# Normalizing attention in groups of three, and converting early weights inside the attention loop

## The chip, the cores and the metric

The kernel runs on one core of a Trainium2 chip. The metric is the time of one execution on the device, in microseconds. Before the change the median of three runs is 826.88 us (826.86 to 827.37). The core's engines run side by side, each through its own list of instructions in order: TensorE (PE: matmuls; PEld: its weight loads), VectorE (DVE), ScalarE (ACT), GpSimd (POOL) and SyncE (SP), which here only issues DMAs. An instruction that reads what another engine writes waits for a semaphore, and everything behind it on its engine waits too.

## The reference

An attention in which a query sees only the keys of its own bucket, and two layers of gated experts behind it. Inputs of the second part are 64-bit floats.

```python
q_bits = (einsum('bhsd,dk->bhsk', q, proj) > 0)      # 6 bits: the bucket; k_bits likewise
mask = q_bucket[:, :, :, None] == k_bucket[:, :, None, :]
scores = where(mask, scale * q @ k.T, -1e9)          # 2 x 8 heads, 768 x 768, head size 64
attn = exp(scores - max(scores)); attn /= attn.sum(-1) + 1e-09
x = (attn @ v) as 1536 tokens x 512
x = (sigmoid(x @ w_gate) * (x @ w_val)) @ w_out      # inner size 1536
h = x @ w_in; out = (h * cos(h)) @ w_out             # inner size 2048
```

A row of `attn` whose bucket holds no key becomes uniform, 1/768.

## The kernel before

**Attention.** A head has 6 groups of 128 query rows, so there are 96 groups `g`. One pass of the loop at `for g in range(NG + LAG + 2)` is a *step*: it works on several groups at once, each in another stage, and within a step the list `ORDER` (in the first steps `FILL`) gives the order in which the stages issue their instructions. That order is final, since the scheduler is told to keep it. The stages of a group:

- `S`: four matmuls write the scores (`scores`, L399 and L402), two steps ahead of the group's own step, negated, with the mask added as a large number by extra rows of the matmul; `MIN`: their row minimum on VectorE (`rowmax`, L406);
- `COEF` (L411): one VectorE operation turns the minimum into scale and bias of the exponential, (-1, minimum), or (0, 0) for a row without a key; `EXP` (L425): the exponential on ScalarE, with the row sum beside it;
- `GRD` (L432) and `RCP` (L438): the sum plus 1e-9, and its reciprocal, on VectorE; `NRM` (L442): GpSimd multiplies the group's 128 x 768 values by it, in place;
- for three groups together, LAG steps later, in 6 half steps `w` of 128 keys: `Ta`/`Tb` transposes on TensorE (L451, tile `t`), `HIa`/`HIb` the high part on ScalarE (L456, `ph`), `LOa`/`LOb` the low part on VectorE (L461, `pl`), `PVa`/`PVb` the products with the values on TensorE (L471 and L472, tile `o`).

With `LAG = 5` the step of group g holds the products of half steps 2(g-5) and 2(g-5)+1. `FIN` copies a finished product (`e`, L480) and sends halves of it across partitions by DMA (L486 to L489); once a pair of heads is done, GpSimd adds them (`ef`, L494) behind the second DMA, and ScalarE and GpSimd write high and low part to `xy` (L510, L514).

Beside it the heads ahead are prepared by a table of due steps (`LOAD_AT`, `TRANS_AT`, `BITS_AT`, `VALUES_AT`): loads, transposes (L286), high and low part (L301, L302 and L305, tile `x`), bucket bits (L360, L363) and the values' two parts (L267, L270, tile `vs`). `PREP` starts what is due, `LATE` runs its second half in the next step.

**Weights.** A weight tile of 128 x 512 arrives as 64-bit words. `convert` turns it to 32 bits: one ScalarE operation (L151) and three on VectorE (L153, L156, L165). `wsplit` makes a high part on ScalarE (L123) and a low part on VectorE or GpSimd (L124). The first six tiles (`NEARLY`) are loaded from step 86 on; four are converted in steps 97 to 100, where only products are left, the other two at the beginning of the second part.

**Second part.** Products of gate, value and output weights, all on TensorE (L670, L732, L759). The scheduler keeps the order within each part; where the end of the first meets the beginning of the second it may place the second's instructions among the first's.

Of the kernel before, what the change touches and what calls it, by code (L numbers as in the profile page):

```python
# [39 lines left out]
def lsh_attention_glu_moe_cos_moe(  # L40
# [190 lines left out]
    def attention():  # L231
        with ExitStack() as st:
# [172 lines left out]
            def rowmax(g):  # L405
                nc.vector.tensor_reduce(mm[:, g % NM, 1:2], s_t[g], axis=AX.XY, op=ALU.min)  # L406

            def coef(g):
                m = mm[:, g % NM, :]
                cb = tiny.tile([P, 2], F32, tag="cb", name=f"cb{g}")  # L410
                nc.vector.scalar_tensor_tensor(  # L411
                    out=cb,
                    in0=m[:, 1:2].to_broadcast([P, 2]),
                    scalar=CUT,
                    in1=m,
                    op0=ALU.is_lt,
                    op1=ALU.mult,
                )
                cb_t[g] = cb

            def expo(g):
                pt = pp.tile([P, 2, HS], F32, tag="p", name=f"p{g}")
                sm = tiny.tile([P, 1], F32, tag="sm", name=f"sm{g}")
                cb = cb_t.pop(g)
                nc.scalar.activation(  # L425
# [426 lines left out]
```

## Time and profile before

| | us |
|---|---|
| median of three runs | 826.88 |
| profiled execution, its own time | 826.57 |
| its span, first to last instruction | 824.8 |
| TensorE busy | 798.6 (97%) |
| VectorE busy | 609.1 (74%) |
| ScalarE busy | 469.1 (57%) |
| GpSimd busy | 312.3 (38%) |

Shares are means over parts with different limits: VectorE's 74% is 99% in the attention and less behind it. A matmul's end is modelled, so where TensorE is called busy it may still be held up for a moment; the start of a matmul that comes once in every step shows that better. "Idle before" in a row is time in which the engine stood, with what ended it.

### The profile page before, as it was taken

The numbers are of one execution on the slowest core, as the hardware profiler recorded it, in microseconds if no ns is written. First come the engines' busy times: TensorE is split into PE (matmuls) and PEld (weight loads), VectorE is DVE, ScalarE is ACT, GpSimd is POOL, SyncE is SP. The second block draws the span as 40 slices with busy tenths as digits, with TensorE's granted clock in tenths as the row PEclk, the third lists the DMA queues.
The fourth block names the chain that finished last, engine by engine and source line by source line (L and its number), as shares of the span: only waits on it lengthen the run. The fifth ranks groups of instructions, "written<-read, shape, count | busy, mean of one in ns | idle before, by whom it ended". The sixth has DMA issues, their size and how long they took to land.

```text
span 824.8 us, 12075 instructions
## 1 busy us (share of the span) xinstructions
PE 798.6 (97%) x3984; PEld 676.8 (82%) x3984; DVE 609.1 (74%) x1157; ACT 469.1 (57%) x896; POOL 312.3 (38%) x315
## 2 busy tenths in 40 slices
PE   7999999999986999999999999999999999999998
PEld 5899999899974888888888888887888888868886
DVE  7999999999998255555454357787777777787773
ACT  5899989888985233223222244456666666664442
POOL 5678878777743112111211112131222222222221
PEclk9999999999997999999999999999999999999999
DMA  7676667576515132223222103232333232243212
GB/s 178 144 167 151 148 152 180 124 169 166 153 30 183 41 103 77 76 82 98 96 83 77 41 36 103 90 115 76 103 103 92 89 101 83 97 137 119 86 68 102
DMA packets 69070, 89.06 MB, mean 108 GB/s; under 512 B 29520, under 2 KB 52048, under 8 KB 69008
## 3 DMA queue, kind: packets, MB, share of 16 engines
q1 hardware_dynamic: 68208, 88.10, 37.6%
q8 instruction: 31, 0.51, 0.3%
q14 instruction: 31, 0.25, 0.1%
q10 hardware_dynamic: 800, 0.20, 0.1%
HBM read 59.77 MB, written 3.15 MB: 76 GB/s over the span
## 4 chain that ended last, share of the span: by engine, by line
PE 81%; DVE 9%; issue 3%; ACT 3%; DMA 2%; POOL 1%; SPq 0%; DVEq 0%; POOLq 0%; ACTq 0%
PE a L759 15%; PE ph L670 14%; PE pg L670 12%; PE pv L670 12%; PE a L732 12%; PE t L451 5%; PE o L471 2%; PE o L472 2%; PE s L399 2%; PE s L402 2%; DVE pl L461 2%; PE pb L360 1%; DVE cb L411 1%; DMA e<-e 1%; ACT p L425 1%
## 5 line engine op out<-in xcount | busy, mean ns | idle before, releaser
L670 PE MATMUL ph<-xy,ih 128*128 128x512 f32 x384 | 118.3, 389 | 0.0
L123 ACT CAST gh<-g 128x512 fp32r<-128x512 f32 x84 | 52.1, 620 | 113.4 <-PE a L759 44.8
L124 POOL TENSOR_TENSOR zl<-w_z,zh 128x512 fp32r<-128x512 f32 x32 | 41.8, 1307 | 169.5 <-ACT zh L123 169.5
L425 ACT ACTIVATE p<-s,cb 128x768 f32<-128x768 f32 x96 | 96.1, 1001 | 13.1 <-DVE cb L411 6.8
L456 ACT CAST ph<-t 128x384 fp32r<-128x384 f32 x192 | 90.8, 485 | 16.1 <-PE t L451 12.1
L696 DVE TENSOR_TENSOR g<-pv,sg 128x512 f32<-128x512 f32 x36 | 24.8, 690 | 99.3 <-PE pv L670 99.3
L451 PE MATMUL t<-ident,p 128*128 128x128 f32 x576 | 94.7, 273 | 3.3 <-DVE pl L461 3.2
L461 DVE TENSOR_TENSOR pl<-t,ph 128x384 fp32r<-128x384 f32 x192 | 96.4, 540 | 1.8 <-ACT ph L456 0.8
L442 POOL TENSOR_SCALAR p<-p,r 128x768 f32<-128x768 f32 x96 | 87.0, 908 | 26.1 <-DVE r L438 12.8
L406 DVE TENSOR_REDUCE mm<-s 128x1 f32<-128x768 f32 x96 | 90.7, 945 | 0.5 <-PE s L402 0.5
L670 PE MATMUL pg<-xy,gh 128*128 128x512 f32 x288 | 90.6, 396 | 0.0
L670 PE MATMUL pv<-xy,vh 128*128 128x512 f32 x288 | 89.1, 391 | 0.0
L694 ACT ACTIVATE sg<-pg 128x512 f32<-128x512 f32 x36 | 21.3, 592 | 117.8 <-PE pg L670 117.8
L451 PEld LDWEIGHTS t<-ident,p 128*128 128x128 f32 x576 | 73.8, 140 | 13.9 <-DVE pl L461 6.5
L670 PEld LDWEIGHTS ph<-xy,ih 128*128 128x128 f32 x384 | 72.0, 188 | 15.1
L124 DVE TENSOR_TENSOR gl<-g,gh 128x512 fp32r<-128x512 f32 x84 | 59.8, 714 | 32.7 <-ACT gh L123 30.5
L471 PE MATMUL o<-ph,vs 128*128 128x384 f32 x192 | 80.5, 419 | 1.5 <-ACT e L480 1.5
L759 PE MATMUL a<-zh,gh 128*128 128x512 f32 x192 | 75.0, 391 | 1.1 <-ACT gh L123 0.4
L759 PE MATMUL a<-zl,gh 128*128 128x512 f32 x192 | 75.0, 390 | 0.7 <-POOL zl L124 0.7
L759 PE MATMUL a<-zh,gl 128*128 128x512 f32 x192 | 74.8, 390 | 0.0
L670 PE MATMUL ph<-xy,il 128*128 128x512 f32 x192 | 74.7, 389 | 0.0
L472 PE MATMUL o<-pl,vs 128*128 128x384 f32 x192 | 65.8, 343 | 6.8 <-DVE pl L461 6.8
(107 smaller groups left out, 1860.8 us busy)
## 6 DMA issues: line engine op xcount, KB each, us to landing
raw_z<-in_moe_w_out SPq DMA_DIRECT2D x32, 512.0 KB, 3.2
raw_o<-in_moe_w_out SPq DMA_DIRECT2D x24, 512.0 KB, 3.2
q<-x SPq DMA_DIRECT2D x45, 192.0 KB, 3.1
k<-x SPq DMA_DIRECT2D x45, 192.0 KB, 3.4
raw_i<-in_moe_w_in SPq DMA_DIRECT2D x16, 512.0 KB, 3.8
raw_g<-in_moe_w_gate SPq DMA_DIRECT2D x12, 512.0 KB, 3.5
raw_v<-in_moe_w_val SPq DMA_DIRECT2D x12, 512.0 KB, 3.7
nv<-in_v SPq DMA_DIRECT2D x8, 384.0 KB, 3.5
```

Source lines behind the costliest of these rows:

```text
L124: sub.tensor_tensor(out=dst_l, in0=src, in1=dst_h.bitcast(F32), op=ALU.subtract)
L406: nc.vector.tensor_reduce(mm[:, g % NM, 1:2], s_t[g], axis=AX.XY, op=ALU.min)
L425: nc.scalar.activation(pt, s_t.pop(g), AF.Exp, bias=cb[:, 1:2], scale=cb[:, 0:1], accum_out=sm)
L442: nc.gpsimd.tensor_scalar(out=pt, in0=pt, scalar1=r_t.pop(g), scalar2=1.0, op0=ALU.mult, op1=ALU.mult)
L451: nc.tensor.transpose(pt[:, i, :], pv_[:, j * P : (j + 1) * P], ident)
L456: nc.scalar.copy(ph, pt_t[w])
L461: nc.vector.tensor_tensor(out=pl, in0=pt_t.pop(w), in1=ph_t[w].bitcast(F32), op=ALU.subtract)
L471: nc.tensor.matmul(o_t[u], vs[:, j, :], ph_t.pop(w), start=(j == 0), stop=False)
L472: nc.tensor.matmul(o_t[u], vs[:, j, :], pl_t.pop(w), start=False, stop=(j == T - 1))
L670: nc.tensor.matmul(ps, w[:, kt, :], xy[c][:, hl, kt, :], start=(n == 0), stop=(n == 11))
L732: nc.tensor.matmul(acc[c, e], w[:, e, :], m, start=(f == 0 and n == 0), stop=(f == F1 - 1 and n == 2),)
L759: nc.tensor.matmul(acc[c, t], m[:, ts], w, start=(f == 0 and n == 0), stop=(f == F2 - 1 and n == 2),)
```

## The change

The minimum goes straight into the exponential as its bias, with scale -1. The small operations are done for three groups at once, on tiles of 128 x 3, at the beginning of every third step: the sum plus 1e-9 (`r`), a number `d` that is 1/768 for a row without a key and else 0, the reciprocal, and `r` set to 0 where the row has no key. `NRM` then normalizes three groups one after the other, as `p * r + d`. `LAG` is 7, so products come two steps later; values are loaded and split later in the table; tiles `p` have 10 buffers instead of 8. `convert` becomes a generator that stops twice: from step 26 on, every tenth step starts one of the six early weights, and the next two steps do its other two pieces. Loads begin at step 16.

```diff
 ORDER = (
-    "Tb LOa PVb EXP Ta MIN GRD LATE COEF RCP W HIb PVa S NRM FIN HIa PREP PVaF LOb".split()
+    "Tb LOa COEF PVb EXP Ta MIN LATE W HIb PVa S NRM FIN HIa PREP PVaF LOb".split()
 )
...
-LOAD_AT = {"q": -17, "k": -19, "v": -13}
+LOAD_AT = {"q": -17, "k": -19, "v": -6}
...
-VALUES_AT = (-8, -6)
+VALUES_AT = (-3, -1)
...
-    def convert(key):
+    def convert_parts(key):
...
             out=lt, in0=lw, scalar1=29, scalar2=7, op0=ALU.logical_shift_right, op1=ALU.bitwise_and
         )
+        yield
...
             op1=ALU.bitwise_or,
         )
+        yield
...
-            pp = st.enter_context(tc.tile_pool(name="pp", bufs=8))
-            tiny = st.enter_context(tc.tile_pool(name="tiny", bufs=6))
+            pp = st.enter_context(tc.tile_pool(name="pp", bufs=10))
+            tiny = st.enter_context(tc.tile_pool(name="tiny", bufs=3))
...
+            def expo(g):
+                u, i = divmod(g, 3)
+                pt = pp.tile([P, 2, HS], F32, tag="p", name=f"p{g}")
+                nc.scalar.activation(
+                    pt,
+                    s_t.pop(g),
+                    AF.Exp,
+                    bias=mn_t[u][:, i : i + 1],
+                    scale=-1.0,
+                    accum_out=sm_t[u][:, i : i + 1],
+                )
+                p_t[g] = pt
+
+            def coef(u):
...
+                nc.vector.tensor_scalar(out=r, in0=sm, scalar1=1e-9, scalar2=None, op0=ALU.add)
+                nc.vector.tensor_scalar(
+                    out=d,
+                    in0=mn,
+                    scalar1=CUT,
+                    scalar2=1.0 / (S + 1e-9),
+                    op0=ALU.is_ge,
                     op1=ALU.mult,
                 )
...
+                nc.vector.reciprocal(r, r)
+                nc.vector.scalar_tensor_tensor(
+                    out=r, in0=mn, scalar=CUT, in1=r, op0=ALU.is_lt, op1=ALU.mult
                 )
...
-                nc.gpsimd.tensor_scalar(
-                    out=pt, in0=pt, scalar1=r_t.pop(g), scalar2=1.0, op0=ALU.mult, op1=ALU.mult
                 )
+            def norm(u):
+                r, d = ra_t.pop(u)
+                for i in range(3):
+                    pt = p_t[3 * u + i]
+                    nc.gpsimd.tensor_scalar(
+                        out=pt,
+                        in0=pt,
+                        scalar1=r[:, i : i + 1],
+                        scalar2=d[:, i : i + 1],
+                        op0=ALU.mult,
+                        op1=ALU.add,
+                    )
...
-            LAG = 5
-            WL = NG - 10
-            WC = (NG + 1, NG + 2, NG + 3, NG + 4)
+            LAG = 7
+
+            WL, WC = 16, 26
+            WSTEP = (NG - WC - 6) // NEARLY
...
-                        if g in WC:
-                            convert_to(1 + WC.index(g))
+                        if done < NEARLY and g >= WC and (g - WC) % WSTEP == 0:
+                            parts = convert_parts(order[done])
+                        if parts is not None and next(parts, parts) is parts:
+                            parts = None
+                            done += 1
                             load_to(done + 3)
...
+                    third = 0 < g <= NG and g % 3 == 0
...
-                convert_to(NEARLY)
```

VectorE in the middle of the loop, before: two steps, each with `pl` twice, the minimum and three small operations.

```order
L461 TENSOR_TENSOR pl_2135<-t_2094,ph_2116 128x384
L461 TENSOR_TENSOR pl_2141<-t_2105,ph_2126 128x384
L406 TENSOR_REDUCE mm<-s_2118 128x1
L432 TENSOR_SCALAR r_2153<-sm_2146 128x1
L411 SCALAR_TENSOR_TENSOR cb_2165<-mm 128x2
L438 RECIPROCAL r_2153<-r_2153 128x1
L461 TENSOR_TENSOR pl_2180<-t_2137,ph_2168 128x384
L461 TENSOR_TENSOR pl_2186<-t_2148,ph_2178 128x384
L406 TENSOR_REDUCE mm<-s_2172 128x1
L432 TENSOR_SCALAR r_2198<-sm_2191 128x1
```

After the change, from step 26 into step 28: the small operations once, and the first two pieces of a weight (L150, L154; `pl` is now L478, the minimum L412, the bits L365).

```order
L365 TENSOR_SCALAR bf_1147<-pb_1148,bcode 64x384
L150 TENSOR_SCALAR wl_g_1178<-raw_g_754 128x512
L478 TENSOR_TENSOR pl_1195<-t_1158,ph_1180 128x384
L478 TENSOR_TENSOR pl_1201<-t_1168,ph_1189 128x384
L435 TENSOR_SCALAR r_1203<-sm_1045 128x3
L436 TENSOR_SCALAR d_1204<-mn_1044 128x3
L444 RECIPROCAL r_1203<-r_1203 128x3
L445 SCALAR_TENSOR_TENSOR r_1203<-mn_1044,r_1203 128x3
L412 TENSOR_REDUCE mn_1172<-s_1184 128x1
L154 SCALAR_TENSOR_TENSOR wl_g_1178<-wp_g_1176,wl_g_1178 128x512
L478 TENSOR_TENSOR pl_1243<-t_1197,ph_1229 128x384
L478 TENSOR_TENSOR pl_1249<-t_1213,ph_1241 128x384
```

The small operations went from every step to every third and ahead of the minimum; the weight's pieces stand at the end of a step, right before the next `pl`.

GpSimd around the addition `ef` of a pair of heads, before: one normalization (`p`) in each step, with the parts of a prepared head between.

```order
L442 TENSOR_SCALAR p_951<-p_951,r_959 128x768
L494 TENSOR_TENSOR ef_653<-e_523,ef_653 128x768
L442 TENSOR_SCALAR p_991<-p_991,r_999 128x768
L442 TENSOR_SCALAR p_1032<-p_1032,r_1040 128x768
L302 TENSOR_SCALAR x_5_926<-xf_1085 128x384
L305 TENSOR_TENSOR x_5_927<-xf_1085,x_5_926 128x384
L442 TENSOR_SCALAR p_1075<-p_1075,r_1083 128x768
```

The same place after the change (`ef` is L511, `p` L454, `x` L304 and L307, `vs` L269 and L272).

```order
L511 TENSOR_TENSOR ef_1143<-e_1017,ef_1143 128x768
L304 TENSOR_SCALAR x_7_1318<-xf_1470 128x384
L307 TENSOR_TENSOR x_7_1319<-xf_1470,x_7_1318 128x384
L454 TENSOR_SCALAR p_1346<-p_1346,r_1455,d_1456 128x768
L454 TENSOR_SCALAR p_1383<-p_1383,r_1455,d_1456 128x768
L454 TENSOR_SCALAR p_1421<-p_1421,r_1455,d_1456 128x768
L269 TENSOR_SCALAR vs_1494<-nv_1371 128x6x64
L272 TENSOR_TENSOR vs_1494<-nv_1371,vs_1494 128x6x64
```

Behind `ef` there now come both parts of `x` and then three normalizations in a row.

TensorE at the end of the attention, before: the last products (`o`), then the first gate product (`pg`).

```order
L471 MATMUL o_4380<-ph_4406,vs_3902 128x384
L472 MATMUL o_4380<-pl_4412,vs_3902 128x384
L471 MATMUL o_4380<-ph_4410,vs_3902 128x384
L472 MATMUL o_4380<-pl_4418,vs_3902 128x384
L471 MATMUL o_4380<-ph_4431,vs_3902 128x384
L472 MATMUL o_4380<-pl_4435,vs_3902 128x384
L670 MATMUL pg_0_4522<-xy_70,gh_0_4493 128x512 x2
L670 MATMUL pg_0_4522<-xy_70,gl_0_4494 128x512
L670 MATMUL pg_0_4522<-xy_70,gh_0_4493 128x512 x2
L670 MATMUL pg_0_4522<-xy_70,gl_0_4494 128x512
```

Some ten half steps before the attention's end, after the change (transposes L468, products L488 and L489, gate product L692).

```order
L468 MATMUL t_4011<-ident,p_3807 128x128
L468 MATMUL t_4011<-ident,p_3838 128x128
L468 MATMUL t_4011<-ident,p_3870 128x128
L488 MATMUL o_3951<-ph_3996,vs_3516 128x384
L692 MATMUL pg_0_4199<-xy_68,gh_0_4172 128x512 x2
L692 MATMUL pg_0_4199<-xy_68,gl_0_4173 128x512
L489 MATMUL o_3951<-pl_4009,vs_3516 128x384
L468 MATMUL t_4019<-ident,p_3807 128x128
L468 MATMUL t_4019<-ident,p_3838 128x128
L468 MATMUL t_4019<-ident,p_3870 128x128
L692 MATMUL pg_0_4199<-xy_68,gh_0_4172 128x512 x2
L692 MATMUL pg_0_4199<-xy_68,gl_0_4173 128x512
```

The first gate product's matmuls moved in among the last transposes and products of the attention.

## Rows read from the trace of the kernel before

**Rows 1.** Busy time by stretch; columns: busy us and count per engine, granted clock, DMA.
```profile
28.10:237.00 208.90, 205.61 (x1373) 191.09 (x1373) 207.15 (x548) 188.40 (x416) 161.32 (x184) 1.00 0.61 148
237.00:247.00 10.00, 7.30 (x49) 6.25 (x47) 7.97 (x23) 8.40 (x19) 4.66 (x5) 1.00 0.09 20
247.00:256.70 9.70, 5.25 (x26) 3.59 (x26) 9.42 (x20) 5.19 (x10) 0.00 (x0) 0.94 0.50 163
256.70:265.50 8.80, 6.50 (x16) 4.63 (x16) 8.45 (x9) 5.15 (x9) 5.53 (x3) 0.50 0.73 225
268.00:824.80 556.80, 551.21 (x2425) 454.19 (x2423) 354.32 (x501) 244.61 (x414) 120.92 (x91) 1.00 0.27 88
```

**Rows 2.** Waits of TensorE, 20 to 268 us: total, times, longest.
```profile
PE o L472 <- DVE pl L461: 6.8, 7, 2.3
```

**Rows 3.** Timeline of TensorE, score starts of groups 6, 8, 54, 56, 57, 60, 95.
```profile
21.61 0.41 PE L399 MATMUL s<-k,q 96*128 96x384 f32 x1 [0.65 <-DMA k<-bf]
...
28.11 0.34 PE L399 MATMUL s<-k,q 96*128 96x384 f32 x1
...
138.17 0.34 PE L399 MATMUL s<-k,q 96*128 96x384 f32 x1
...
143.17 0.34 PE L399 MATMUL s<-k,q 96*128 96x384 f32 x1
...
145.23 0.34 PE L399 MATMUL s<-k,q 96*128 96x384 f32 x1
...
153.47 0.34 PE L399 MATMUL s<-k,q 96*128 96x384 f32 x1
...
236.94 0.34 PE L399 MATMUL s<-k,q 96*128 96x384 f32 x1
```

**Rows 4.** Timeline of VectorE, then GpSimd, around 147 us: start, duration, engine, line.
```profile
145.31 1.00 DVE L461 TENSOR_TENSOR pl<-t,ph 128x384 fp32r<-128x384 f32 x2
146.23 0.94 DVE L406 TENSOR_REDUCE mm<-s 128x1 f32<-128x768 f32 x1
...
147.15 0.66 DVE L363 TENSOR_SCALAR bf<-pb,bcode 64x384 fp32r<-64x384 f32 x1
147.74 1.66 DVE L411 SCALAR_TENSOR_TENSOR cb<-mm 128x2 f32<-128x2 f32 x1
...
147.55 1.83 POOL L494 TENSOR_TENSOR ef<-e,ef 128x768 f32<-128x768 f32 x1 [2.25 <-DMA e<-e]
```

**Rows 5.** Busy time of line 411 alone (`cb`), attention loop.
```profile
28.10:211.50 183.40, 23.18 (x77) 1.00 0.63 151
```

**Rows 6.** Groups of GpSimd instructions, 28.1 to 237 us: count, busy, mean ns.
```profile
L442 POOL TENSOR_SCALAR p<-p,r 128x768 f32<-128x768 f32 x87 | 78.8, 908 | 20.1 <-ACT ph L456 9.4 <-DVE r L438 7.9 <-DMA q<-x 1.7
L305 POOL TENSOR_TENSOR x<-xf,x 128x384 fp32r<-128x384 f32 x26 | 26.5, 1019 | 2.2
L302 POOL TENSOR_SCALAR x<-xf 128x384 fp32r<-128x384 f32 x26 | 13.3, 511 | 8.4 <-ACT xf L301 8.3
```

**Rows 7.** Line 153 over the whole kernel: duration ns min/median/max.
```profile
L153 DVE TENSOR_SCALAR wl_v<-raw_v x12: 415/1534/1540, 247.4 to 441.5; 128x512 int32<-128x512 int32 x12
```

**Rows 8.** Groups of VectorE instructions, 247 to 256.7 us.
```profile
L156 DVE SCALAR_TENSOR_TENSOR wl_v<-wp_v,wl_v 128x512 int32<-128x512 int32 x2 | 1.4, 688 | 0.1
```

**Rows 9.** Timeline of ScalarE and of SP's queue at three moments.
```profile
140.36 0.49 ACT L480 COPY e<-o 128x384 f32<-128x384 f32 x1
...
143.27 0.61 SPq L489 DMA_DIRECT2D e<-e  x1
...
240.05 1.00 ACT L425 ACTIVATE p<-s,cb 128x768 f32<-128x768 f32 x1
```

**Rows 10.** Groups of ScalarE instructions, 237 to 268 us.
```profile
L456 ACT CAST ph<-t 128x384 fp32r<-128x384 f32 x14 | 6.7, 479 | 2.1 <-PE t L451 2.0
...
L123 ACT CAST vh<-w_v 128x512 fp32r<-128x512 f32 x2 | 1.2, 620 | 0.0
```

**Rows 11.** Chain of waits, 255 to 275 us: start, us, what.
```profile
268.06 2.72 PE pg L670 x12
```

More of the change, by code (lines that the diff above doesn't have):

```diff
@@ L84, in constants @@
     def constants():
+        srow = xy[NC - 1].bitcast(F32)[0:1, 0, 0, 0 : 2 * D].rearrange("p (d two) -> p d two", two=2)
         make_identity(nc, ident)
@@ L218, in convert_to @@
             load_to(done + 3)
-            convert(order[done])
+            for _ in convert_parts(order[done]):
+                pass
             done += 1
@@ L231, in attention @@
     def attention():
+        nonlocal done
+        parts = None
         with ExitStack() as st:
@@ L387, in bits @@
                 return evac
-            s_t, p_t, cb_t, sm_t, r_t, o_t, e_t, f_t = ({} for _ in range(8))
+            s_t, p_t, mn_t, sm_t, ra_t, o_t, e_t, f_t = ({} for _ in range(8))
             pt_t, ph_t, pl_t = {}, {}, {}
@@ L405, in rowmax @@
             def rowmax(g):
[L406 to L416, printed above, removed]
+                u, i = divmod(g, 3)
@@ new lines, in rowmax @@
+                if i == 0:
+                    mn_t[u] = tiny.tile([P, 3], F32, tag="mn", name=f"mn{u}")
+                    sm_t[u] = tiny.tile([P, 3], F32, tag="sm", name=f"sm{u}")
+                nc.vector.tensor_reduce(
+                    mn_t[u][:, i : i + 1], s_t[g], axis=AX.XY, op=ALU.min
+                )
+            def expo(g):
+                u, i = divmod(g, 3)
+                pt = pp.tile([P, 2, HS], F32, tag="p", name=f"p{g}")
[8 more added lines that the diff above has]
+                p_t[g] = pt
@@ L417, in coef @@
                     op1=ALU.mult,
                 )
[L419 to L425, printed above, removed]
-                    pt, s_t.pop(g), AF.Exp, bias=cb[:, 1:2], scale=cb[:, 0:1], accum_out=sm
-                )
-                p_t[g], sm_t[g] = pt, sm
-            def guard(g):
-                r = tiny.tile([P, 1], F32, tag="r", name=f"r{g}")
-                nc.vector.tensor_scalar(
-                    out=r, in0=sm_t.pop(g), scalar1=1e-9, scalar2=None, op0=ALU.add
-                )
-                r_t[g] = r
@@ L571, in attention @@
                     nc.sync.dma_start(pj[D * g : D * g + D, :], proj)
-                nc.sync.dma_start(bcode, srow)
+                nc.sync.dma_start(
+                    bcode, xy[NC - 1].bitcast(F32)[0:1, 0, 0, 0 : 2 * D].rearrange("p (d two) -> p d two", two=2)
+                )
                 load(1, "q")
```

25 lines of the change are left out of this document (10 added, 15 removed).

## Prediction

> **What bounds the kernel now.** I first read busy time by stretch [rows 1]. From 268 us to the end TensorE works 551 of 557 us at the full granted clock; the change touches nothing there, it only starts it earlier or later. The attention loop is nearly as full (205.6 of 208.9 us from 28.1 to 237), with VectorE busy 99% beside it. Between them lies a hole: from 237 to 256.7 us TensorE works 12.55 of 19.7 us and GpSimd, from 247 on, not at all; in the next 8.8 us, after the idle time, the granted clock is 0.50, the lower of the two levels (1.2 GHz). Among the waits of TensorE [rows 2] the largest is 6.8 us in seven times on `pl`, which VectorE writes: there the six weight conversions stand between its `pl` operations.
>
> Busy time hides stalls inside the loop, because a matmul's end is modelled. So I go by the start of each group's score matmuls [rows 3]. Three undisturbed steps take 145.23 - 138.17 = 7.06 us, the lightest of them 145.23 - 143.17 = 2.06. The next three end at 153.47: 8.24, so 1.18 lost. Beside it, in the timeline of VectorE and GpSimd [rows 4], the small operation `cb` (two elements a partition) lasts 1.66 us instead of some 0.15 and ends at 149.40; GpSimd's `ef` addition started before it and ends at 149.38. So `cb`, which reads two operands in SBUF, stood until GpSimd's instruction was over. It lost 1.50 and TensorE 1.18: VectorE had 0.32 us of slack in three steps, and needs 6.74 of 7.06. By the distances in rows 4 two `pl` take 0.92, the minimum 146.23 to 147.15 with one small operation 0.92 (0.86 alone, estimate), the bits 0.59 once in three steps; that leaves (6.74 - 3 x 1.78 - 0.59) / 3 = 0.27 for the three small operations of a step. The mean `cb` is 23.18 / 77 = 0.30 us [rows 5], 0.15 more than it needs.
>
> Over the loop: group 8's scores start at 28.11, group 95's at 236.94 [rows 3], 208.8 us for 87 steps. 75 steps at 7.06 / 3 make 176.5, the last twelve, with hardly any head left to prepare, about 12 x 2.06 + 0.5 = 25.2. So 7.1 us are stalls; the rest is TensorE's own floor.
>
> **The change part by part.** The sum is made on the profiled run, 826.57 us, 0.31 under the median of 826.88.
>
> *Start.* Products begin two steps later, so steps 4 and 5 hold no transposes and no products. Group 6's scores start at 21.61 on a DMA that stays; group 8's come 6.5 us later [rows 3], since these steps now carry products. Without them two steps are bounded by the exponential (1.0, [rows 9]) and a head's preparation beside it (as long as `ph`, 0.5, estimate, [rows 10]), and the first transposes wait for three normalizations (3 x 0.91, [rows 6]) queued on GpSimd behind two `x` operations. I put group 8 at 25.6: **-2.5**, bounds 0 and -4. The work left out here comes back at the end and is counted there.
>
> *Small row operations.* In three steps nine become four: 0.81 falls to about 0.36 by the same distances, and the waits of `cb` from three to one of its kind. VectorE's slack in three steps grows from 0.32 to 0.77, and nothing stands between the minimum and the exponential any more. TensorE gains only its stalls: **-7.1** if all vanish, which is the bound on this side; what comes back stands in the next two terms. The normalization gets a second scalar by pointer and an addition. No row shows that form; the copy `x` (0.511 for 384 elements, no pointer) and `p` (0.908 for 768, one pointer) [rows 6] lie on one line of about 1 ns an element, so a pointer has no price there and I take none.
>
> *The six weights.* Each brings VectorE 0.42 + 0.69 + 0.69 = 1.80 us [rows 7, 8] in three consecutive steps, ScalarE one operation (as a weight cast, 0.62, estimate from [rows 10]) and SP one load. What hid them was the hole at the end; in the loop it is the slack, 0.77. They wait for GpSimd too: `wl_v`, 0.415 at the least, has a median of 1.534 in the kernel's second part [rows 7]. In the loop GpSimd is busy 161 of 209 us, where the pieces stood until now 0 of 9.7 [rows 1]. From below: no waits, and the slack of nearly two blocks of three steps: 1.80 - 1.3 = 0.5 a weight, 3 in all. From above: each piece waits out a whole `p` (0.9), with the slack of one block and what was saved up before it (0.32): 1.80 + 2.7 - 1.1 = 3.4, or 20. With the mean wait of `cb` (0.15, the row nearest in kind) 1.80 + 0.45 - 1.1 = 1.15, or 7. I take **+8**: the pieces stand at the end of a step, at other moments than `cb`.
>
> The Trainium skill (SBUF — State Buffer, "SBUF: two separate sides") says that VectorE and GpSimd share a pair of ports under an exclusive lock held for a whole instruction, and that a VectorE operation with two SBUF inputs takes part. Rows 4 agree: 149.40 against 149.38. By that rule a piece waits for the rest of whatever GpSimd runs, on estimate half of 0.9 us in three cases of four, 18 x 0.35 = 6 us; the term would be 10, where `cb`'s mean gives 7.
>
> *GpSimd in bunches.* Three normalizations now come together, behind `x` (0.51 + 1.02, [rows 6]) and, once in twelve steps, behind `ef`, which waits for a DMA. Now the copy `e` starts at 140.36, its second DMA is issued at 143.27 [rows 9] and `ef` starts at 147.55 [rows 4]. After the change no bit DMAs stand ahead of it on SP: the copy 0.49, one other issue 0.6 (estimate, as the one in rows 9), then 4.28 as now: 5.4. Then `ef` 1.83, `x` 1.53, three `p` 2.7: 11.5 us after `e`. The transposes want it five steps after the step of `e`, 5 x 2.35 = 11.8, plus their own place in the step (0.7) less that of `e` (1.4, both estimates from the order): 11.1. So it is late by 0.4 seven times, and by more where a weight load or a piece falls in. SP also stands at the next pair's first `ef` until the low parts of `xy`, now queued behind a bunch, are done. With the wait of the new small operation, **+6**, bounds 1 and 14.
>
> *End.* From group 95's scores to the second gate product it is 268.06 - 236.94 = 31.1 us [rows 3, 11]. After the change one conversion stands there instead of six, and the first gate product's matmuls lie between the attention's. ScalarE is then the longest: the last exponential starts 240.05 - 236.94 = 3.1 after the scores [rows 9]; behind it come the exponential with its sum (1.2, estimate), 15 `ph` x 0.48, five weight casts x 0.62 [rows 10], two copies `e` of 0.49, two casts `xy` and one conversion (1.6, estimates by size): 14.1. With 1.5 for gaps, 0.8 for the last `pl` and product and 2.72 for the value product [rows 11] it is 22.1. TensorE's own part is 18 half steps of about 0.68 (the 2.06 less four score matmuls of 0.175, by half) and twelve gate matmuls of 2.72 / 12: 15.7. So **-9.0**; bounds -6 (ScalarE with larger gaps) and -11.
>
> Sum: -2.5 - 7.1 + 8 + 6 - 9.0 = -4.6; 826.57 becomes 822.0, against the median 822.3. I say 822.5.
>
> **The rivals.**
> 1. *The weights fit in.* 29 blocks x 0.45 = 13 us of VectorE are freed and 6 x 1.80 = 10.8 come in: weights 3, bunches 2. Against it: three pieces come in three steps, then none for seven. 826.6 - 2.5 - 7.1 + 5 - 9 = 813.
> 2. *GpSimd becomes the bound (slower).* The chain `e`, DMA, `ef`, `x`, three `p`, transposes misses its place each twelve steps by 2 us or more, and the pieces, which lock GpSimd out as it does them, push it further: weights 11, bunches 14. For it: 11.5 against 11.1 leaves nothing over. Against it: with single normalizations the same wait costs TensorE no more than what the block of `cb` explains. Then 826.6 - 2.5 - 7.1 + 25 - 9 = 833; it is slower from 18.6 us of new stalls on.
> 3. *What the end gains is spent in the loop*: new stalls of 17 to 20 us, 825 to 828. Here too belongs that the change doesn't do what it says: TensorE is the floor of the loop, so seven steps instead of five between exponential and products free nothing.
>
> **Chances.** Forecast (817 to 825) 0.42, rival 1 0.18, rival 3 0.17, rival 2 0.23. About 0.2% (1.65 us) is what a measurement of this kernel can tell: faster 0.60, within it 0.17, slower 0.23. The forecast's own range is 817 to 825. 814 to 831 leaves about one in ten on each side; the low side takes the weights and bunches near their lower bounds with the end as forecast, the high side both some ten above it together.
>
> **What would show it.** Right: three-step times of 7.06 except around steps 26, 36, 46, 56, 66 and 76, there 1 to 2 us longer, with conversion pieces longer than 0.69; no exponential that waits for a small operation; about 22 us from group 95's scores to the second gate product, at a granted clock of 1.00. Wrong: that stretch above 27; three-step times of 9 every twelve steps with transposes waiting for `p` (rival 2); pieces of 0.69 and no longer steps (rival 1).

## The result and the profile after

The changed kernel takes 834.16 us (833.83 to 835.7, 4 runs) against 827.04 for the kernel before on the same chip: ratio 1.0089, interval 1.0072 to 1.0107. It is slower, by 7.1 us; I had forecast 822.5. The profiled execution's span is 832.0 us against 824.8, so the traces show the whole difference.

Three moments split it. Group 8's scores start at 24.73 us instead of 28.11 [rows 3], group 95's at 254.85 instead of 236.94, the second gate product at 275.26 instead of 268.06 [rows 11]. So the start gives 3.4 us, the end 10.7 (20.4 us instead of 31.1), and the loop between takes 230.1 instead of 208.8: 21.3 us lost, more than both gains. The two score starts, and from the chain of waits the gate product:

```profile
24.73 0.42 PE L401 MATMUL s<-k,q 96*128 96x384 f32 x1
...
254.85 0.34 PE L401 MATMUL s<-k,q 96*128 96x384 f32 x1
...
275.26 2.72 PE pg L692 x12
```

Busy time by stretch, to be held against [rows 1] (columns as there):

```profile
24.70:254.90 230.20, 212.96 (x1371) 194.36 (x1372) 212.96 (x421) 189.53 (x421) 174.93 (x186) 0.99 0.64 153
254.90:275.30 20.40, 19.79 (x119) 16.77 (x118) 15.31 (x31) 16.68 (x36) 13.40 (x11) 1.00 0.17 43
275.30:832.00 556.70, 551.13 (x2424) 454.18 (x2422) 356.23 (x501) 245.82 (x416) 125.82 (x94) 1.00 0.27 88
```

The hole at the end is closed: TensorE works 19.8 of 20.4 us at full clock, and the part behind is as before. The loss is in the loop. Three undisturbed steps still take 7.07 us; the long ones stand singly between them. The one that loses most begins with group 22's scores, 6.72 us instead of 2.40. Its timeline, SP's queue first, then VectorE, TensorE and GpSimd:

```profile
50.42 0.71 SPq L133 DMA_DIRECT2D raw_g<-in_moe_w_gate  x1
51.17 0.65 SPq L133 DMA_DIRECT2D raw_v<-in_moe_w_val  x1
51.87 0.66 SPq L133 DMA_DIRECT2D raw_g<-in_moe_w_gate  x1
...
56.64 0.60 SPq L506 DMA_DIRECT2D e<-e  x1
...
61.04 0.67 DVE L365 TENSOR_SCALAR bf<-pb,bcode 64x384 fp32r<-64x384 f32 x1 [3.87 <-DMA k<-bf]
...
61.77 0.55 PE L288 MATMUL pt<-ident,nqk 128*128 128x128 f32 x3 [3.05 <-DVE bf L365]
...
65.53 1.83 POOL L511 TENSOR_TENSOR ef<-e,ef 128x768 f32<-128x768 f32 x1 [8.24 <-DMA e<-e]
67.33 0.52 POOL L304 TENSOR_SCALAR x<-xf 128x384 fp32r<-128x384 f32 x1
```

Three weights, 1.5 MB, are issued ahead of the copies of the bits (`bf`) and of `e`. The bits' buffer comes free late: VectorE stands 3.87 us, TensorE 3.05. The second copy of `e`, issued at 56.64, lets `ef` start only at 65.53: 8.9 us, in [rows 4, 9] 4.3. Behind `ef` on GpSimd stand `x` and three `p`. Busy time by stretch there shows two more things:

```profile
54.00:58.70 4.70, 4.70 (x32) 4.19 (x30) 2.97 (x5) 4.03 (x10) 3.29 (x4) 1.00 1.08 316
58.70:61.70 3.00, 0.02 (x1) 0.00 (x0) 0.66 (x2) 0.37 (x2) 0.00 (x0) 1.00 1.16 241
61.70:63.50 1.80, 1.73 (x10) 1.49 (x10) 1.76 (x8) 1.01 (x2) 0.00 (x0) 0.74 1.15 183
63.50:66.00 2.50, 2.50 (x10) 2.40 (x10) 1.51 (x3) 1.37 (x3) 0.47 (x1) 0.50 0.32 50
```

The DMA share (last column but one) is above 1 while the copies are under way, against 0.64 over the loop. And after TensorE's 3 us of idle its granted clock falls to 0.50, the lower level (1.2 GHz), so the wait is followed by slower matmuls until 66: 1.7 us are lost (estimate, 0.26 of 1.8 and 0.50 of 2.5). The loop has one more stretch like it, after waits of 1.8 us and less; its 0.23 of 7.5 us are another 1.7, some 3.4 in all. First that stretch, then the whole loop:

```profile
131.00:138.50 7.50, 5.21 (x23) 4.33 (x23) 5.92 (x9) 3.34 (x9) 7.42 (x7) 0.77 0.47 116
33.61:254.85 221.24, 204.14 (x1314) 186.35 (x1313) 204.35 (x405) 181.72 (x404) 168.14 (x179) 0.98 0.63 152
```

The waits of TensorE over the loop, against [rows 2] (total, times, longest), and of GpSimd at `ef`:

```profile
PE o L489 <- DVE pl L478: 4.5, 5, 1.7
PE pt L288 <- DVE bf L365: 3.0, 1, 3.0
PE pb L362 <- POOL x L304: 2.7, 3, 1.8
...
PE pb L362 <- POOL x L307: 2.1, 4, 0.5
...
POOL ef L511 <- DMA e<-e: 16.1, 4, 8.2
POOL ef L511 <- DMA ef<-e: 8.9, 2, 4.8
```

GpSimd stands 25 us at `ef`, and what TensorE waits for behind it is `x`, for the bits product `pb`. The other new thing is the weights' pieces on VectorE, against [rows 7, 8] (count, busy, mean ns):

```profile
L150 DVE TENSOR_SCALAR wl_g<-raw_g 128x512 int32<-128x512 int32 x2 | 2.9, 1456 | 0.0
L154 DVE SCALAR_TENSOR_TENSOR wl_o<-wp_o,wl_o 128x512 int32<-128x512 int32 x2 | 2.1, 1066 | 0.0
```

All 18 together take 16.0 us where, at the shortest durations in [rows 7, 8], they would take 10.8.

### The profile page after: what moved, and what is told of

It is laid out like the page before. It is cut to its first block, busy times and chain, and to the rows that moved or that the text cites. A ratio compares the mean times of both kernels' runs of the same rounds, so it can differ in the third digit from the quotient of the medians.

```text
span 832.0 us, 11799 instructions
## 1 busy us (share of the span) xinstructions
PE 800.7 (96%) x3984; PEld 677.4 (81%) x3984; DVE 603.1 (72%) x996; ACT 466.5 (56%) x896; POOL 327.9 (39%) x315
## 4 chain that ended last, share of the span: by engine, by line
PE 75%; DVE 8%; ACT 6%; issue 4%; DMA 3%; POOL 3%; SPq 0%; ACTq 0%; POOLq 0%; DVEq 0%
PE a L781 15%; PE ph L692 13%; PE pv L692 12%; PE a L754 12%; PE pg L692 12%; PE t L468 4%; ACT p L419 2%; PE o L489 2%; DVE mn L412 2%; DVE pl L478 2%; PE o L488 2%; PE s L401 2%; DMA e<-e 2%; PE s L404 1%; ACT ph L473 1%
## 5 line engine op out<-in xcount | busy, mean ns | idle before, releaser
L692 PE MATMUL ph<-xy,ih 128*128 128x512 f32 x384 | 118.1, 389 | 0.0
L478 DVE TENSOR_TENSOR pl<-t,ph 128x384 fp32r<-128x384 f32 x192 | 101.2, 550 | 10.7 <-ACT ph L473 9.8
L454 POOL TENSOR_SCALAR p<-p,r,d 128x768 f32<-128x768 f32 x96 | 99.5, 1048 | 3.0 <-PE o L489 2.8
L468 PE MATMUL t<-ident,p 128*128 128x128 f32 x576 | 95.9, 276 | 4.6 <-ACT xf L303 2.2
L412 DVE TENSOR_REDUCE mn<-s 128x1 f32<-128x768 f32 x96 | 91.1, 949 | 1.3 <-PE s L404 1.2
L419 ACT ACTIVATE p<-s,mn 128x768 f32<-128x768 f32 x96 | 87.7, 914 | 5.5 <-DVE mn L412 5.2
L692 PE MATMUL pg<-xy,gh 128*128 128x512 f32 x288 | 89.2, 389 | 0.0
L692 PE MATMUL pv<-xy,vh 128*128 128x512 f32 x288 | 88.7, 389 | 0.0
L468 PEld LDWEIGHTS t<-ident,p 128*128 128x128 f32 x576 | 73.5, 141 | 14.7 <-issue 3.0
L716 ACT ACTIVATE sg<-pg 128x512 f32<-128x512 f32 x36 | 21.4, 594 | 114.0 <-PE pg L692 114.0
L692 PEld LDWEIGHTS ph<-xy,ih 128*128 128x128 f32 x384 | 72.1, 188 | 14.9
L488 PE MATMUL o<-ph,vs 128*128 128x384 f32 x192 | 79.5, 414 | 0.3 <-ACT e L497 0.3
L692 PE MATMUL ph<-xy,il 128*128 128x512 f32 x192 | 74.7, 389 | 0.0
L401 PE MATMUL s<-k,q 96*128 96x384 f32 x192 | 69.3, 361 | 3.2 <-ACT p L419 2.7
```

Source lines behind the costliest of these rows:

```text
L401: nc.tensor.matmul(o, hh["q2"][0:96, t, :], hh["k2"][0:96, sl, :], start=True, stop=False)
L412: nc.vector.tensor_reduce(mn_t[u][:, i : i + 1], s_t[g], axis=AX.XY, op=ALU.min)
L419: nc.scalar.activation(pt, s_t.pop(g), AF.Exp, bias=mn_t[u][:, i : i + 1], scale=-1.0, accum_out=sm_t[u][:, i : i + 1],)
L454: nc.gpsimd.tensor_scalar(out=pt, in0=pt, scalar1=r[:, i : i + 1], scalar2=d[:, i : i + 1], op0=ALU.mult, op1=ALU.add,)
L468: nc.tensor.transpose(pt[:, i, :], pv_[:, j * P : (j + 1) * P], ident)
L478: nc.vector.tensor_tensor(out=pl, in0=pt_t.pop(w), in1=ph_t[w].bitcast(F32), op=ALU.subtract)
```

## Experiments

Theory A: the weights' loads delay the copies that `ef` and `bf` wait for, and `x` and three `p` queue behind `ef`. Theory B, later called D: the pieces cost VectorE's time, under D because it has none to spare. Rival C: three `p` in a row are dear by themselves. The measure is the time from group 12's scores to group 95's ("loop") and from there to the second gate product ("end"), in the profiled run; times are medians, ratios are to the kernel before, timed beside it.

A step whose length is given is named by the group whose scores begin it; the loop issues these two steps ahead, so step 22 lies in step 20 of the code. Loads, pieces and the copy `e` are named by the code's step, as in the edits; the second copy `e` of a pair comes at 19, 31, 43 and so on. A landing is counted from the issue of that copy's second DMA to the start of `ef`.

| kernel | loop | TensorE busy in it | end | us | ratio, 95% |
|---|---|---|---|---|---|
| before | 199.7 | 196.4 | 31.1 | 827.0 | |
| changed | 221.2 | 204.1 | 20.4 | 834.2 | 1.0089 (1.0072 to 1.0107) |
| e1 `ef` later | 213.0 | 200.7 | 20.4 | 827.9 | 1.001 (0.9997 to 1.0022) |
| e2 weights at end | 199.0 | 196.8 | 33.8 | 825.4 | 0.9979 (0.997 to 0.9988) |
| e3 weights only | 218.8 | 204.5 | 18.7 | 832.9 | 1.0069 (1.0053 to 1.0085) |
| e4 single loads | 215.2 | 202.4 | 22.7 | 832.7 | 1.0086 (1.0057 to 1.0115) |
| e5 loads only | 215.7 | 204.6 | 33.7 | 840.6 | 1.0168 (1.0129 to 1.0206) |
| e6 pieces only | 212.9 | 200.7 | 34.2 | 841.1 | 1.0169 (1.0154 to 1.0184) |
| e7 reductions | 207.2 | 199.2 | 33.3 | 843.8 | 1.0206 (1.0188 to 1.0223) |
| e8 spread | 207.1 | 197.9 | 20.4 | 820.1 | 0.9915 (0.9901 to 0.993) |
| e9 in step | 245.1 | 215.4 | 22.9 | 863.4 | 1.0434 (1.0411 to 1.0456) |
| e10 spread, `ef` as before | 209.4 | 199.7 | 22.7 | 826.2 | 0.9988 (0.9979 to 0.9997) |
| e11 in step, rows | 242.3 | 212.4 | 23.2 | 862.4 | 1.0435 (1.0411 to 1.0459) |
| e12 load earlier | 205.4 | 198.4 | 23.2 | 821.5 | 0.9936 (0.9923 to 0.995) |
| e13 same, rows | 211.2 | 202.5 | 20.4 | 824.8 | 0.9976 (0.9964 to 0.9987) |
| e14 a period earlier | 206.7 | 199.0 | 23.1 | 822.4 | 0.9939 (0.9921 to 0.9957) |
| e15 `ef` in three | 206.0 | 198.3 | 20.4 | 819.8 | 0.9914 (0.9898 to 0.993) |
| e16 both | 208.0 | 197.9 | 21.4 | 821.2 | 0.9932 (0.9916 to 0.9948) |

**e1_sum_later.**

```diff
-SUM_AT, HIGH_AT, LOW_AT = 1, 5, 5
+SUM_AT, HIGH_AT, LOW_AT = 2, 5, 5
```

> The changed kernel with one number changed: the sum ef of a pair of heads is issued on GpSimd one step later, behind x and the three small p of that step (SUM_AT 2 for 1). Theory A (GpSimd stands at ef for its DMA, and the x that the bits matmul pb wants and the three p queue behind it; the long steps 22, 24, 36, 38, 48, 50, 59 and 84, 17 us together): the waits of ef for its DMAs fall from 25 us to under 5, those steps lose most of it, and the time is 834 - 12 to 14 = 820 to 822 us. Theory B (the pieces of the six weights, stretched while GpSimd works, are what made the loop long): 832 to 835, as the changed kernel, since no piece moves. Theory C (three p in a row are dearer by themselves, 0.976 us each against 0.89, and whatever is behind them is late wherever ef stands): 830 to 834, the long steps only move.

Measured 827.9, between A and B. Steps 36, 48, 59 and 84 lose 1.5, 4.1, 2.0 and 1.25 us; group 22's step stays (7.28), now on `bf` alone. At 48 and 84 the copy had landed late in the changed kernel (6.2 and 4.9 us), as A says; at 59 it had not (3.3), and e6 below has steps 36 and 59 as long with no load at all. 13.9 us over e2 are left.

**e2_weights_at_end, e3_weights_only.** The two halves of the change by themselves.

```diff
-            WL, WC = 16, 26
-            WSTEP = (NG - WC - 6) // NEARLY
+            WL = NG - 10
+            WC = (NG + 1, NG + 2, NG + 3, NG + 4)
```

(e2; with it `convert_to` in the loop's end and behind it, as before. e3 is the same edit the other way round in the kernel before.)

> The changed kernel with the six weights put back: loaded at step 86 and converted at steps 97 to 100 and behind the loop, as in the kernel before. What is left of the change is the small row operations for three groups and the seven steps. The stretch from group 95's scores to the second gate product grows again by about 9.5 us (31 - 20.4 = 10.7 at most). Theory A (the waits are made by ef, and the weights have a part in it only by their three loads at step 16, which hold up the DMAs of the first sum): the loop gives back 4 to 5 us, so 834 - 4.5 + 9.5 = 839. Theory B (the weights' pieces lengthen the loop): it gives back 12 to 14, so 834 - 13 + 9.5 = 830.

> The kernel before with the weights' part alone: loaded from step 16, converted in three pieces each from step 26 on; small operations for each group, five steps, values and orders as they were. Theory A: with one p in a row GpSimd is not late at ef, the pieces fit beside the matmuls at under 4 us, and the end gains 9.5: 827 - 9.5 + 3 = 820 to 821. Theory B: the pieces cost 12 to 14 us in the loop whatever p does: 827 - 9.5 + 13 = 830. My prediction's own term for the weights, 8 us: 825.

e2 is faster than before, by 0.2%, and C falls. Its loop takes 199.0 us, TensorE busy for 196.8:

```profile
34.30:233.32 199.02, 196.80 (x1315) 184.74 (x1312) 190.89 (x387) 177.38 (x398) 160.48 (x178) 1.00 0.63 153
```

The third `p` ends 10.6 us after `e` and nothing waits for it. e3's loop is 19.1 us longer than before's, with single `p`: the weights cost nearly the same whatever the small operations do. The loop loses 22.2 us to them in the new order (221.2 - 199.0), the end gives back 13.4 (33.8 - 20.4).

**e4_loads_single.**

```diff
-                        if g == WL:
-                            load_to(3)
+                        if g >= WL and (g - WL) % WSTEP == 0:
+                            load_to(min((g - WL) // WSTEP + 1, NEARLY))
```

(WL is 22; the next three weights are loaded after the last conversion.)

> The changed kernel with the weights' loads one at a time, four steps ahead of each conversion (steps 22, 32, 42, 52, 62, 72) instead of three at step 16. Theory A: the first sum's DMAs, which now land 8.9 us after their issue behind 1.5 MB of weights, land in about 4, group 22's and 24's long steps (+4.3 and +1.0) go for the most part, and the later periods stay: 834 - 4 = 830. Theory B and C: 833 to 835; the loads do not matter.

Group 22's long step is gone (2.40) as A says. But steps 48, 60 and 84 are 1.9 to 4.6 us longer, each behind a landing of 5.3 to 6.9 us: loads come at step 42, one before an `e`, at 52, and three at 78. The loop gains 6.1 us, the end loses 2.3, and the time gains only 1.5.

**e5_loads_only, e6_pieces_only, e7_reduces.** Each adds one thing to e2.

```diff
+                        if g == 16:
+                            for key in order[3:6]:
+                                load_raw(key)
+                        if g in (28, 38, 48, 58, 68, 78):
+                            load_raw(order[(g - 28) // 10 % 3])
...
```

(e5)

> The kernel of e2_weights_at_end (weights converted at the end, 825.4 us) with loads of weights at the steps of the changed kernel: three at step 16 and one each at steps 28, 38, 48, 58, 68 and 78; the first six fetch weights that nothing reads, the last three those that the end wants, and nothing is loaded at step 86. No piece of a conversion runs in the loop. From group 12's scores to group 95's it took 199.0 us in e2 and 221.2 in the changed kernel. Theory A (the loads hold up the DMAs that ef and bf wait for, and x and the three p stand behind ef): 199 + 8 to 11 = 207 to 210 us, the first long step at group 22 with about +4, and 834 us in all. Theory D (the loads are free, VectorE has no time for the pieces): 199 to 201 us, and 825 to 827 in all.

```diff
+                        if 26 <= g < 86 and (g - 26) % 10 < 3:
+                            k, part = divmod(g - 26, 10)
...
+                                nc.vector.scalar_tensor_tensor(
+                                    out=z["l"], in0=z["p"].bitcast(I32), scalar=3, in1=z["l"],
...
```

(e6: the three pieces on spare tiles; e7: `nc.vector.tensor_reduce(w, z["p"], axis=AX.X, op=ALU.min)` for each)

> The kernel of e2_weights_at_end with the 18 pieces (and six ScalarE steps) of six conversions run in the loop at the steps of the changed kernel, from three weights loaded once at step 8; what they make is not used, and the end converts its weights as e2 does. No load stands near a sum ef. Theory D (VectorE, 190.9 us busy of 199.0 in e2 with its records end to end, has no room for 6 x 1.8 us and their stretching by GpSimd): 199 + 9 to 12 = 208 to 211 us from group 12's scores to group 95's, about 836 in all. Theory A (the loads alone make the long steps): 199 to 202 us, 826 to 828 in all. Both halves real: this run's and e5's excess add up to about the 22 us of the changed kernel.

> As e6_pieces_only, with each of the 18 pieces replaced by a reduction of 128x512 numbers to one column, which reads one tile and should take about 0.6 us whatever GpSimd does (the loop's reductions of 128x768 take 0.94 to 0.95 beside GpSimd's p); so VectorE gets about as much to do, 18 x 0.6 = 11 us, without the stretching. Theory D in its plain form (VectorE's time is what is short): 208 to 211 us from group 12's scores to group 95's, as e6. If it is the stretching by GpSimd that costs: 3 to 6 us less than e6.

Loads alone cost 16.7 us of loop, more than I expected of A. `ef` in the first two disturbed periods, on GpSimd:

```profile
66.95 1.82 POOL L511 TENSOR_TENSOR ef<-e,ef 128x768 f32<-128x768 f32 x1 [8.65 <-DMA e<-e]
...
99.25 1.81 POOL L511 TENSOR_TENSOR ef<-e,ef 128x768 f32<-128x768 f32 x1 [5.44 <-DMA ef<-e]
```

The granted clock of this loop is 0.97, in e2 1.00: by it some 6.5 us of the 16.7 (estimate, 3% of 216) are slower matmuls after the waits.

```profile
34.64:250.33 215.69, 204.56 (x1315) 188.84 (x1313) 190.70 (x387) 178.11 (x398) 160.56 (x178) 0.97 0.65 156
```

Pieces alone cost 13.8 us, and last 13.5 in all (the groups on VectorE):

```profile
L643 DVE SCALAR_TENSOR_TENSOR zl<-zp,zl 128x512 int32<-128x512 int32 x6 | 5.6, 936 | 0.0
L649 DVE SCALAR_TENSOR_TENSOR zw<-raw_g,zl 128x512 int32<-128x512 int32 x4 | 3.0, 759 | 0.0
L638 DVE TENSOR_SCALAR zl<-raw_g 128x512 int32<-128x512 int32 x4 | 2.0, 504 | 0.0
L638 DVE TENSOR_SCALAR zl<-raw_v 128x512 int32<-128x512 int32 x2 | 1.6, 817 | 0.0
L649 DVE SCALAR_TENSOR_TENSOR zw<-raw_v,zl 128x512 int32<-128x512 int32 x2 | 1.3, 674 | 0.0
```

Reductions of nearly the same length, 12.1 us, cost 8.2, so 5.6 less: VectorE's plain time is the larger part, and the rest goes with what the pieces share with GpSimd, which is busy 7 us longer in e6 and not in e7 (160.5 in e2). The loops of e6 and e7, GpSimd's busy time in the fifth place:

```profile
34.20:247.06 212.86, 200.68 (x1314) 184.07 (x1313) 203.84 (x405) 181.95 (x404) 167.72 (x178) 1.00 0.56 138
34.59:241.76 207.17, 199.16 (x1315) 184.07 (x1313) 199.61 (x405) 181.25 (x404) 160.82 (x179) 1.00 0.58 142
```

A and D are both right; 16.7 and 13.8 make 30.5, not 22.2, so the two do not add. Step 36, for one, takes 7.35 us with loads alone, 4.57 with pieces alone and 4.58 with both; why both together cost less than the sum is not shown. (e7 is read by its loop alone: behind the gate products it is 9.4 us longer, which the last section comes to.)

Two of the long steps stand in e6 too, so no load is needed for them. Step 59 is 3.92 us there and 3.64 in the changed kernel, with `ef` on time: `ef` falls on the last small operation, and a piece stands behind it, so that the next `pl` is late. In the changed kernel, on VectorE, GpSimd and TensorE:

```profile
162.10 1.74 DVE L445 SCALAR_TENSOR_TENSOR r<-mn,r 128x3 f32<-128x3 f32 x1
...
164.63 1.30 DVE L154 SCALAR_TENSOR_TENSOR wl_v<-wp_v,wl_v 128x512 int32<-128x512 int32 x1
...
161.99 1.83 POOL L511 TENSOR_TENSOR ef<-e,ef 128x768 f32<-128x768 f32 x1 [1.96 <-DMA e<-e]
...
166.46 0.44 PE L489 MATMUL o<-pl,vs 128*128 128x384 f32 x1 [1.74 <-DVE pl L478]
```

At step 36 the copy lands late in both, 5.2 us, in e6 with no weight under way; what delays it there is open.

**e8_spread.**

```diff
-            WL, WC = 16, 26
-            WSTEP = (NG - WC - 6) // NEARLY
+            WL, WC, WSTEP = 20, 24, 9
...
+                        if WL <= g < WL + 6 * WSTEP and (g - WL) % WSTEP == 0:
+                            load_to((g - WL) // WSTEP + 1)
...
-                        if parts is not None and next(parts, parts) is parts:
+                        if parts is not None and g % 3 == 0 and next(parts, parts) is parts:
```

(with e1's edit)

> The changed kernel with three changes: the sum ef one step later (as e1), the weights' loads one at a time at steps 20, 29, ... 65 with the next three at step 86, and the 18 pieces one every third step from 24 to 75 (at the steps where no bits are taken out) instead of three in a row every ten. Theory A and D together: the late landings cost nothing and a single piece of 0.6 us is partly made up before the next one, so from group 12's scores to group 95's 199 + 4 to 7 = 203 to 206 us with the short end of the changed kernel: 834 - 15 to 18 = 816 to 819 us. If a piece costs its time wherever it stands: 199 + 11 = 210 us, 823 in all.

820.1 us, 0.85% faster than before and 14 us faster than the changed kernel. Of its 8.1 us over e2 nearly all stands in one step a period. There, on VectorE, GpSimd and TensorE:

```profile
97.29 1.82 DVE L435 TENSOR_SCALAR r<-sm 128x3 f32<-128x3 f32 x1
...
97.26 1.83 POOL L511 TENSOR_TENSOR ef<-e,ef 128x768 f32<-128x768 f32 x1
...
101.72 0.44 PE L489 MATMUL o<-pl,vs 128*128 128x384 f32 x1 [1.57 <-DVE pl L478]
```

`r`, three elements a partition, ends within 0.02 us of `ef`: moving `ef` a step had put it on the small operations, as `cb` in [rows 4]. A piece of 0.83 us stands in the same step before the `pl` that TensorE waits for. Three of the first six copies still take 4.3 to 5.9 us from issue to landing here, but `ef`, a step later, finds them landed.

**e9_in_step, e10_spread_sum1, e11_rows.** e9 and e11 differ from e8 by `SUM_AT` 1 and `WL, WC, WSTEP = 21, 24, 12` (e11 without `g % 3 == 0`), with the next three weights loaded at 93; e10 by `SUM_AT` 1 alone.

> The changed kernel with its sum ef where it was (SUM_AT 1) and the weights in step with the periods of twelve: one load at steps 21, 33, ... 81, two steps after each pair's e, and one piece each at steps 24, 27, 30 of every period; the three loads of the next weights at step 93. In e8 the six steps lengthened by 1.2 to 1.7 us each (8 us in all) are those where ef, issued a step later, holds GpSimd for 1.83 us while the small operation r on VectorE stands (r 1.82 us for 0.16); elsewhere e8 runs at the pattern of e2. So with ef back before x and with its DMA free of loads: 199 + 1 to 3 us from group 12's scores to group 95's, 820 - 6 = 813 to 815 us. If the loads two steps after e still hold its DMA up, or single pieces do cost their time: 818 to 822.

> e8_spread with the sum ef back at SUM_AT 1: loads every nine steps (20, 29, 38, 47, 56, 65), of which those at 20, 29 and 56 lie within two steps of an e (19, 31, 55). If ef's place behind x was worth something only because of late DMAs, and loads near an e make them late: e8's 8 us at r go, but two or three of the periods lose 1 to 4 us at ef, so 815 to 820 us, above e9. If single loads do no harm: as e9, 813 to 815.

> e9_in_step with the three pieces of a weight in a row again (steps 24, 25, 26 of each period, as in the changed kernel) instead of one every third step; loads as in e9. If what a piece costs is its own time because VectorE has no room within three steps (e6: 13.5 us of pieces, 13.8 us of excess): e9 + 6 to 12 = 820 to 826 us. If the place of a piece does not matter: as e9.

e9 failed by my placing: SP's queue and ScalarE, first period:

```profile
66.44 0.60 SPq L348 DMA_DIRECT2D k<-x  x1
67.08 0.59 SPq L133 DMA_DIRECT2D raw_g<-in_moe_w_gate  x1
...
73.42 0.68 ACT L148 ACTIVATE wp_g<-raw_g 128x512 f32<-128x512 f32 x1 [6.03 <-DMA raw_g<-in_moe_w_gate]
```

A load issued by the program three steps ahead stood on SP behind six copies that wait for `x`, and left when ScalarE already wanted it; ScalarE's `ph` stood behind. e11 fails alike and tells nothing of rows. e10 shows A once more: its steps 36, 48 and 72 lose 4.1, 1.6 and 1.3 us, behind the loads at 29, 38 and 65, two to five steps before an `e` (landings of 5.0 to 6.3 us).

**e12_two_later, e13_rows_later.** `WL, WC, WSTEP = 22, 27, 12`; e12 with `g % 12 in (0, 3, 6)`, e13 without a condition.

> e9_in_step with time for the load: the weight's load at steps 22, 34, ... 82 (three steps after each e), its pieces at steps 27, 30 and 36 of each period (not where ef runs). In e9 the load was issued on the DMA queue behind the six copies of x at 67.08 us, ScalarE reached the conversion at 67.4 and stood 6.0 us until it landed; that made the steps of 8.7 and 4.9 us, once a period, 45 us in all, while a step with a single piece was longer than in e2 by 0.03 to 0.2 us. So with the load landed before its first piece and ef's DMA free of loads: from group 12's scores to group 95's 199 + 1 to 3 us, 813 to 816 us in all, below e8's 820. If single pieces cost their 0.7 us: 199 + 12, 823.

> As e12, with the three pieces of a weight at steps 27, 28 and 29, in a row as in the changed kernel. If VectorE has no room for three pieces within three steps (e6: 13.5 us of pieces, 13.8 us of excess over e2; e7: 12.1 and 8.2): 6 to 12 us above e12. If in e6 and e7 it was the place of single weights beside ef or the bits that cost, and not the row: within 3 us of e12.

The first six landings are now 3.2 to 3.3 us in both, in e2 3.1 to 3.5. The row costs 5.8 us of loop (211.2 against 205.4), just under the 6 to 12 of D, at a clock of 1.00 in both; of the time it costs 3.3, since e13's end is 2.8 shorter. e12 came out above its 813 to 816: 6.4 us of its loop stay over e2, and its end is 23.2.

**e14_period_earlier, e15_sum_in_three, e16_earlier_in_three.** e14 is e12 with `WL, WC, WSTEP = 10, 15, 12`; e15 is e8, e16 is e14, with

```diff
-                nc.gpsimd.tensor_tensor(out=xf, in0=e_t.pop(hd - 1), in1=xf, op=ALU.add)
+                e = e_t.pop(hd - 1)
+                for c in range(0, S, 256):
+                    nc.gpsimd.tensor_tensor(
+                        out=xf[:, c : c + 256], in0=e[:, c : c + 256], in1=xf[:, c : c + 256], op=ALU.add
+                    )
```

> e12_two_later with the weights one period earlier: loads at steps 10, 22, ... 70, pieces from step 15 to 84. e12 took 23.2 us from group 95's scores to the second gate product, where the changed kernel and e8 took 20.4, because its last pieces and the next weights' loads stand at steps 87 to 96. With these gone: the loop as e12 (205 us from group 12's scores), the end 2.8 us shorter, 818 to 819 us. If the end's 2.8 us come from elsewhere: 821 to 822, as e12.

> e8_spread with the sum ef as three instructions of 256 columns in place of one of 768 (1.83 us). In e8 the small operation r on VectorE ends with ef, 1.82 us for 0.16, in each of six periods. If VectorE and GpSimd exclude each other for one whole instruction: r waits for a third only, 0.6 us, each of the six steps gets 1.1 to 1.2 us shorter, GpSimd's 0.1 us an instruction more beside it: 820 - 5 to 7 = 813 to 815 us. If GpSimd keeps what they share through all of its consecutive instructions, or the long step has another cause: 820 as e8.

> e14_period_earlier with the sum in three pieces. In e12 an r of 1.75 us that ends with ef made a step 1.1 us longer in three periods, and waits of pieces and r for other work the rest. Exclusion by single instructions: 2 to 4 us below e14, 814 to 817 us. Otherwise as e14.

e14's end stays at 23.1, so the pieces and loads that stood there in e12 are not its cause. Its trace shows another: the attention's last copy but one lands in 4.4 us (5.0 in e12, 3.2 in e13), `ef` and the `p` behind it are late, and TensorE waits 0.6 us for them and 1.3 for `pl`, where e13 waits 0.3 in all for these.

```profile
247.57 0.33 PE L468 MATMUL t<-ident,p 128*128 128x128 f32 x1 [0.64 <-POOL p L454]
```

The other ends of 22.7 to 23.2 with loads in the loop (e4, e9, e10, e11) have this landing at 4.4 to 5.0 too; those of 20.4 have it at 3.2, or `ef` a step later. Why it varies is open: in e2, with no load near, it is 4.3. In e15 the exclusion is by single instructions, as expected; VectorE and GpSimd at the same place as in e8:

```profile
97.43 0.69 DVE L436 TENSOR_SCALAR d<-mn 128x3 f32<-128x3 f32 x1
...
98.24 0.58 DVE L445 SCALAR_TENSOR_TENSOR r<-mn,r 128x3 f32<-128x3 f32 x1
...
97.33 2.15 POOL L513 TENSOR_TENSOR ef<-e,ef 128x256 f32<-128x256 f32 x3
```

`r` is back at 0.15, but `d` and the last `r` now wait for a third each, so most long steps get 0.7 to 1.0 us shorter instead of 1.2; and steps three further on grow by 0.8, where VectorE, now earlier, meets GpSimd's `xy` (`r` 0.71) and `x` (a piece 1.24). The time is e8's. The price was right for one operation and the sum wrong, because the next operation in line meets the next instruction of GpSimd.

The Trainium skill (SBUF — State Buffer, "SBUF: two separate sides") has GpSimd and some VectorE operations exclude each other for a whole instruction. e8 and e15 agree: 1.82 us beside one instruction of 1.83, at most 0.69 beside three that take 2.15.

## Why the prediction was wrong

*Start*, -2.5: -3.4 measured. Right.

*End*, -9.0: -10.7. Right that the hole closes; the path was another. I had taken ScalarE for the longest, but it is busy 16.7 us, and TensorE itself works 19.8 of the 20.4; that the number came near is in part luck.

*Old stalls*, -7.1: too large. With the small operations alone (e2) the loop gains 0.7 us from group 12 on. The long steps of `cb` went, but 0.82 us a period stay (29.09 us for twelve steps where the first undisturbed twelve take 28.26); my floor had none.

*GpSimd in bunches*, +6: with the old stalls this makes -1.1, and e2 has -0.7 from group 12 on, so the two came out right together by luck, each alone too large. The chain from `e` was 10.6 us where I had put 11.5, and nothing waits for it. The second pointer costs something: `p` 985 ns in e2 against 908 [rows 6]; GpSimd has room for it. From e2's groups:

```profile
L454 POOL TENSOR_SCALAR p<-p,r,d 128x768 f32<-128x768 f32 x84 | 81.7, 985 | 4.2 <-PE o L489 4.2
```

*The six weights*, +8 within 3 to 20: this step failed. They cost 22.2 us of loop (changed against e2), 19.1 with single operations (e3). The working priced the pieces on VectorE alone and wrote "SP one load" without a price. The loads alone cost 16.7 us (e5), through DMAs that `ef` and `bf` wait for. My upper bound for the pieces held (13.8 in e6); that of the term did not, because the loads, and the lower clock after the long waits (some 3.4 us), stood in no bound of it. The row that I gave for pieces that wait, `wl_v` with a median of 1.534 [rows 7], was also one-sided: the other four groups of that line have medians of 0.417 to 0.420. By group 12's and 95's scores the measured parts add up: -3.6 at the start, -0.7 + 22.2 in the loop and -10.7 at the end make 7.2, the difference of the spans.

*Rival 2* named the time, 833, and the sign, but only part of the cause. GpSimd's chain by itself fits (e2); it is late mainly where a copy under the weights' loads is. That the pieces hold GpSimd up and it holds them up is in e6 (7 us of its busy time; step 59). I had written that a weight load would make it later, and gave that no microsecond. The first to wait was not the transposes for `p` but `pb` for `x`. What I had named as signs was half right: 7.07 for undisturbed three steps and 20 us at the end, but long steps at 22, 48 and 59 beside those of the pieces. Rival 1's sign, pieces of 0.69 without longer steps, does not appear in the changed kernel; rival 3 was too small.

## What to carry to other kernels

A load that moves into a full loop is priced by what shares its transfers and its queue: list every copy issued within a few steps of it, and who waits for each. Fillers for an engine that has 4% to spare go in one at a time; three in a row cost about their length here (13.8 us for 13.5). A small VectorE operation that fell on GpSimd's `ef` lasted until that was over (1.66, 1.74 and 1.82 us here, for 0.15), so the place of a long GpSimd instruction is part of the price. Split a change into its halves first: here one gains 0.2%, and with the other spread and `ef` a step later the two gain e8's 0.85%.

## What was not expected of the hardware

A wait of TensorE can cost more than its length: 3.05 us at 58.7 were followed by granted clocks of 0.74 and 0.50 until 66.

In e7 the matmuls behind the loop that read `xy` take 394 ns instead of 389; the groups of e7, then of e2:

```profile
L699 PE MATMUL ph<-xy,ih 128*128 128x512 f32 x384 | 120.5, 394 | 0.0
```

```profile
L688 PE MATMUL ph<-xy,ih 128*128 128x512 f32 x384 | 118.4, 389 | 0.0
```

Only a tile of one column was added; that it shifts the tiles behind it to addresses that read more slowly is a guess, not tried. And the exponential, whose scale is now a number instead of a column, takes 0.91 us, where it took 1.00 [rows 9].
